# Sparse attention and a Mish MLP on one core: half of batch 0's strided q and k loaded as fp32 by SyncE, local v behind them, batch 1's local v cast in flight, and the loads of every block held behind a mark

## Chip, cores and metric

The kernel runs on one core of one Trainium2 chip. The metric is the device time of one execution in microseconds. TensorE is called PE, VectorE DVE, ScalarE ACT, GpSimd POOL and SyncE SP. ACT and SP issue hardware DMAs, which copy without a change of type. POOL issues software DMAs, which in this kernel also cast fp32 to bf16 in flight.

## The reference, cut to what matters

```python
# q, k, v: (8 batches, 8 heads, 576 positions, 64) in fp32
rel = pos[:, None] - pos[None, :]
mask_local   = (rel >= 0) & (rel < 32)                                  # heads 0 to 3
mask_strided = (rel >= 0) & (pos[None, :] % 32 == pos[:, None] % 32)    # heads 4 to 7
attn_out = softmax(where(mask, q @ k.T / 8, -1e9)) @ v

# x: attn_out as (4608 tokens, 512); w_in: (512, 2048); w_out: (2048, 512)
h = x @ w_in
g = h * tanh(softplus(h))        # Mish
out = g @ w_out                  # (4608, 512) in fp32
```

## The kernel before

Attention goes by batches of 576 positions, the MLP by nine blocks of 512 tokens (`t` = 0 to 8). Attention of batch `t + 1` is woven into the second matmul (`w_out`) of block `t`, one step of a list after each step of the MLP. The order of all instructions is written out by hand (`manual_schedule`), so on each engine, and on each engine's DMA queue, program order is execution order. Semaphores keep the data right.

Strided heads lie as 72 partitions of 8 positions, local heads as 96 positions in each of 6 windows. A local window also needs the 32 positions before it, so `vl` holds 128 partitions a window: 96 of its own and 32 that repeat the end of the window before. q and k are needed with the head dimension on partitions. Batches 0 and 1 transpose them on PE (`t_step`), batches 2 to 7 by DMA transposes that SP issues (`transpose_by_dma`, lines L224 and L230: one each for strided k and q, `kTs` and `qTs`, then two each for local k and q, `kTl` and `qTl`, the last of them writing `qTl`).

**Start.** SP loads strided k of heads 4 and 5 as fp32 into `st0`, which DVE casts, and local v of heads 0 and 1 as fp32 into `vl32` (L868, L871), which POOL casts (L898). POOL's queue loads, with a cast in flight, the other strided k heads, all strided q, strided v, local k and q (L126, L154, L147), then local v of heads 2 and 3 (L893), the first two quarters of `w_in` (L184), and, behind the cast of v and a memset (L899), the last two quarters. PE runs `unread` matmuls, whose results nobody reads, between the first transposes. When the strided scores, the local scores and the local products with v (`pv2`, L369) are through, the dense matmuls of block 0 (L522) begin.

**Block 0.** POOL goes on with `w_out` and batch 1's q, k and strided v. SP loads batch 1's local v as fp32 (L171) once a small `gate` DMA, which reads the third quarter of `w_in`, could be issued (L940); POOL casts it during the second half of the block.

**Blocks 1 to 7.** The first matmul (`mlp1`) is seven products of quarters in place of eight (lines L553, and L522 for the rest), the second as well (L749). In the step `fourth` of block `t`, POOL issues the loads of the next batch's local v (`load_own_v_loc`, four DMAs, L175), then strided v of batch `t + 2`, and at the first step of the second matmul strided k and q of batch `t + 2` (L126). In block 1 alone POOL first copies four elements of `qTl` to `mark` (L628): it waits there for the last DMA transpose of batch 2, and the loads wait behind it. ACT copies the 32 repeated rows of v from the window before (`share_v_loc`, L181) at the eighth step of the second matmul. Late in the block POOL casts local k and q of batch `t + 2` (L199), which SP loaded as fp32 (L140), and SP transposes them. POOL also masks the local scores (L353).

Of the kernel before, what the change touches and what calls it, by code (L numbers as in the profile page):

```python
# [10 lines left out]
F32 = mybir.dt.float32  # L11
# [5 lines left out]
NW = 6  # L17
# [3 lines left out]
CS, PN = 8, 72  # L21
# [22 lines left out]
def kernel(ctx, tc, q, k, v, moe_w_in, moe_w_out, out):  # L44
    nc = tc.nc
    B, H, S, D = q.shape
# [78 lines left out]
    def load_str(b, dst, src, h0=0):  # L125
        nc.gpsimd.dma_start(  # L126
            dst[b % 2][0:PN, h0:4, :], src[b, 4 + h0:8].rearrange("h (p j) d -> p h (j d)", j=CS)
        )
# [47 lines left out]
                vl[b % 2][32:128, :, h, 0:D], v[b, h].rearrange("(w p) d -> p w d", p=WQ)  # L176
            )

    def share_v_loc(b):
        x = vl[b % 2]  # L180
        nc.scalar.copy(x[0:32, 1:NW, :, 0:D], x[96:128, 0:NW - 1, :, 0:D])  # L181

    def load_w_in(f0, f1):
        nc.gpsimd.dma_start(  # L184
            w_in[:, :, f0:f1], moe_w_in.rearrange("(cc p) f -> p cc f", p=128)[:, :, f0:f1]
        )
# [8 lines left out]
    def cast(eng, out_, in_):  # L195
        if eng is nc.scalar:
            nc.scalar.copy(out_, in_)  # L197
        else:
            eng.tensor_copy(out_, in_)  # L199

    def load_tiles_loc(b, dst, src):
        to = by_tile(dst[0])
        for h in range(4):
            nc.gpsimd.dma_start(
                to[:, h // 2, :, h % 2, :], src[b, h].rearrange("(i p) d -> p i d", p=PL)
            )
# [38 lines left out]
    def t_step(b, kind, which, hp, eng=None):  # L245

        eng = eng or nc.vector
        tr = tile_t("tr")[:].bitcast(BF16)
        if kind == "s":
            src = (qs if which == "q" else ks)[b % 2]  # L250
            for u in range(8):
                h, jj = 2 * hp + u // 4, u % 4
                nc.tensor.transpose(
                    tr[:, PN * u:PN * u + PN],
                    src[0:PN, h, 128 * jj:128 * jj + 128],
                    ident[0:PN, 0:PN],
                )
            dst = (qTs if which == "q" else kTs)[:, 8 * SU * hp:8 * SU * hp + 8 * SU]
            cast(
                eng, dst.rearrange("c (u n) -> c u n", u=8)[:, :, 0:PN],  # L260
                tr[:, 0:S].rearrange("c (u n) -> c u n", u=8),
            )
        else:
            src = by_head((ql if which == "q" else kl)[b % 2])
            for j in range(CL):
                for e in range(2):
                    nc.tensor.transpose(  # L267
                        tr[64 * e:64 * e + 64, PL * j:PL * j + PL],
                        src[:, 2 * hp + e, D * j:D * j + D], ident[0:PL, 0:PL],
                    )  # L270
            dst = qTl[:, hp, :] if which == "q" else kTl[:, hp, 32:32 + S]
            cast(
                eng, dst.rearrange("c (p j) -> c p j", j=CL),
                tr[:, 0:S].rearrange("c (j p) -> c p j", j=CL),
            )

    def unread(n, i_acc=None):

        tr = tile_t("un")[:] if i_acc is None else acc(i_acc, "un")[:, 0, :]
        for _ in range(n):  # L280
            nc.tensor.matmul(tr, lhsT=zeros[:, 0:128], rhs=zeros, start=True, stop=True)
# [224 lines left out]
    def mlp1(t, accs):  # L506
# [83 lines left out]
        y = {}  # L590
# [28 lines left out]
        def fourth():  # L619
            product(z[2], 0, a22, t4, last=True)  # L620
            for n in range(2):
                mish(z[2][n], 1, 0, 2 * n)
            if t == 1:
                sums_w()[2](slice(4, 8))
                sums_w()[3](slice(0, 4))
            sums_g(gT, 0, 4, "12")
            if t == 1:
                Po.tensor_copy(mark[:], qTl[0:1, 1, S - 4:S])  # L628
            if t < B - 1:
                load_own_v_loc(t + 1)  # L630
            if t < B - 2:
                load_early_v_str(t + 2)
# [228 lines left out]
    with tc.manual_schedule():  # L861
# [1 line left out]
        Sc.preload_act_table(AF.Exp)  # L863
        Sc.dma_start(consts[:], consts_h.ap())
        st0 = g_pool.tile([128, 16, 512], BF16, tag="gT", name="st0")
        st0 = st0[0:PN].rearrange("p a b -> p (a b)").bitcast(F32)[:, 0:1024].rearrange("p (h x) -> p h x", h=2)
        nc.sync.dma_start(st0, k[0, 4:6].rearrange("h (p j) d -> p h (j d)", j=CS))
        nc.sync.dma_start(vl32[32:128, 0, 0, :], v[0, 0, 0:96, :])  # L868
        first = v[0, 0:1, 0:1, :].offset + 64 * D
        heads = vl32[:].rearrange("p h w d -> p (h w) d")  # L870
        nc.sync.dma_start(heads[:, 1:12, :], bass.AP(v.tensor, first, [[D, 128], [WQ * D, 11], [1, D]]))  # L871
        load_str(0, ks, k, 2)
        load_str(0, qs, q)
        load_early_v_str(0)
        load_early_loc(0)
        Dv.memset(zeros, 0.0)
# [8 lines left out]
        for i in range(2):  # L885
            Dv.memset(vs[i][:, :, :, D:D + 1], 1.0)
            Dv.memset(vl[i][:, :, :, D:D + 1], 1.0)
        for i in range(2):
            Dv.memset(vl[i][0:32, 0, :, D:D + 1], 0.0)

        for h in (2, 3):
            first = v[0, h:h + 1, 0:1, :].offset - 32 * D
            nc.gpsimd.dma_start(  # L893
                vl[0][:, :, h, 0:D], bass.AP(v.tensor, first, [[D, 128], [WQ * D, NW], [1, D]])
            )
        load_w_in(0, 512)
        load_w_in(512, 1024)
        cast(Po, vl[0][:, :, 0:2, 0:D], vl32[:, 0:2].rearrange("p h w d -> p w h d"))  # L898
        Po.memset(vl[0][0:32, 0, :, 0:D], 0.0)  # L899
        load_w_in(1024, 1536)  # L900
        load_w_in(1536, 2048)
        for x in (ks, qs):
            Po.memset(x[1][64:SU].rearrange("p h x -> p (h x)").bitcast(F32), 0.0)

        a = Attn(0)
        unread(16)
        cast(Dv, ks[0][0:PN, 0:2, :], st0)
        t_step(0, "s", "k", 0, Sc)
        unread(3, 2)
        t_step(0, "s", "k", 1, Sc)  # L910
        ps = [a.bias("s", i, i) for i in range(2)]
        unread(5, 2)
        t_step(0, "s", "q", 0, Sc)
        t_step(0, "s", "q", 1, Dv)
        unread(2, 2)
        ps.append(a.bias("s", 2, 2))
# [19 lines left out]
        load_early_v_str(1)  # L936
        load_w_out(1, 2)
        load_early_loc(1)
        load_w_out(2, 4)
        nc.sync.dma_start(gate[:], w_in[0:1, 0, 1024:1280])  # L940
        load_v_loc(1)
        accs = (1, 0, 2)
        gT, g1s, g1 = mlp1(0, accs)
        a.pv2("l", 0, 1)
# [17 lines left out]
        for t in range(NBLK):  # L962
            if t == 0:
                x, y, z = accs
                at, ts = attn_steps(1, y, y)
                at[3] += [
                    lambda: load_early_v_str(2), lambda: load_tiles_loc(2, kl, k),
                    lambda: cast_v_loc(1, Po), lambda: load_tiles_loc(2, ql, q),
                ]
                at[12].append(lambda: transpose_by_dma(2))  # L970
                at[1].append(lambda: sums_w()[0](lo))
                at[7].append(lambda: sums_w()[0](hi))
                at[9].append(lambda: sums_w()[1](lo))
                at[11].append(lambda: sums_w()[1](hi))
                at[14].append(lambda: sums_x(1, "1"))
                at[15] += [
                    lambda: spread_v_str(2, Dv),
                ]
                out_accs = (z, x)
            else:  # L980
                if t == 1:
                    split_third()
                x, y = 0, 1
                gT, z, g1 = mlp1(t, (y, x) if t == 1 else (x, y))
                at = attn_steps(t + 1, x, y) if t + 1 < B else []
                if t == 1:
                    at[0].append(lambda: sums_w()[3](hi))
                if t + 2 < B:
                    at[10].append(lambda: transpose_by_dma(t + 2))
                if t + 1 < B:  # L990
                    at[7].append(lambda: share_v_loc(t + 1))
                if t + 2 < B:
                    at[0].append(lambda: load_qk_str(t + 2))
                if t + 1 < B:
                    at[12].append(lambda: sums_x(t + 1, "1"))
            for i, g in enumerate(g1):
                g()
                if t == 0:
                    for s in ts if i == len(g1) - 1 else ():
                        s()  # L1000
                    continue
            if t == 0:
                steps = mlp2(t, gT, out_accs, fc_major=True)
            elif t == NBLK - 1:
                mlp2_last(t, gT, z[5])
                break
            else:
                za, zc = [bank(i, "pso")[:].rearrange("p (n o) -> p n o", n=2) for i in range(2)]
                steps = mlp2_seven(t, gT, z[5], za, zc)
                if t + 1 == B:  # L1010
                    steps[12] = lambda f=steps[12]: (sums_x(t + 1, "1"), f())
            for i, g in enumerate(steps):
                g()
                if i < len(at):
                    for s in at[i]:
                        s()
                if t > 0 and i == 9 and t + 2 < B:
                    cast_qk_loc(t + 2, Po, Po)
            if t < B - 3:
                load_qk_loc(t + 3)  # L1020
# [30 lines left out]
```

## Time and profile before

| | |
|---|---|
| median of 3 runs | 288.06 us (287.17 to 288.32) |
| the profiled execution | 290.55 us, span 288.8 us |
| PE busy | 279.3 us, 97% of the span |
| PE weight loads, ACT, DVE, POOL busy | 219.3, 196.6, 190.8, 105.3 us |
| granted clock of PE | 0.993 on the mean |
| DMA | 40.73 MB, 141 GB/s; HBM read 37.20 MB, written 9.44 MB |
| packets under 512 bytes | 86396 of 103965 |

Times in the profile are from the start of the span. Block `t` begins with its first dense matmul: block 0 at 21.6, block 1 at 57.4, block 2 at 86.5, block 3 at 119.9 us. A row of the timeline has start, length, engine, line, operation, what it writes and reads, how often, and in brackets how long the engine had been idle and what ended that. A row of DMA issues has the size that one DMA writes and the time from issue to landing. In the DMA view q0 is POOL's software queue and q1 SP's hardware queue, with packets, MB written and the share of the 16 engines' time that their packets took; these overlap, so a share can pass 100%.

### The profile page before, as it was taken

Reading aid. Unit: us, or ns where it says so; the run is one execution under the profiler, and the core shown is the slowest. Engines: PE = TensorE matmul, PEld = TensorE weight load, DVE = VectorE, ACT = ScalarE, POOL = GpSimd, SP = SyncE. Lnnn points to the kernel's source line nnn. Section 1 sums busy time; section 2 is a strip of 40 time slices with the busy share of each in tenths; the row PEclk is TensorE's granted clock in tenths of the full one; section 3 lists DMA queues with packets and bytes.
Section 4 is the critical chain, followed back from the end, with each engine's and each line's share of the span. In section 5 each row is a group of like instructions: output and inputs, shape, how many; then the busy total and the mean of one; then the engine's idle time right before and its main releaser. Section 6 shows DMA issues by size and latency. Waiting matters only on the chain.

```text
span 288.8 us, 7515 instructions
## 1 busy us (share of the span) xinstructions
PE 279.3 (97%) x3106; PEld 219.3 (76%) x3121; DVE 190.8 (66%) x403; ACT 196.6 (68%) x292; POOL 105.3 (36%) x122
## 2 busy tenths in 40 slices
PE   8999999999999969999999999999999999999995
PEld 3564455686898648977898889778977897788684
DVE  2273167889786737768776777687868776735742
ACT  2578643699857947689758985898589858506920
POOL 8375536307396015910691069306710600000000
PEclk9999999999999979999999999999999999999999
DMA  8999999999979999999999999999993032003004
GB/s 158 185 205 190 193 194 199 145 137 241 171 102 116 130 257 160 144 235 152 161 109 123 218 151 139 143 227 151 160 149 113 1 137 47 0 3 145 0 2 145
DMA packets 103965, 40.73 MB, mean 141 GB/s; under 512 B 86396, under 2 KB 99436, under 8 KB 103932
## 3 DMA queue, kind: packets, MB, share of 16 engines
q1 hardware_dynamic: 67900, 25.13, 57.1%
q0 software_dynamic: 35744, 14.87, 46.8%
q8 instruction: 24, 0.39, 0.6%
q10 hardware_dynamic: 288, 0.25, 0.3%
q14 instruction: 9, 0.07, 0.1%
HBM read 37.20 MB, written 9.44 MB: 162 GB/s over the span
## 4 chain that ended last, share of the span: by engine, by line
PE 87%; DMA 7%; DVE 2%; ACT 1%; POOL 1%; issue 1%; SPq 0%; ACTq 0%; POOLq 0%
PE pso L749 30%; PE psu L553 10%; PE psh L522 9%; PE psv L553 8%; PE psb L553 7%; PE po L369 4%; PE pso L809 4%; PE psb L522 4%; PE pso L782 4%; DMA qTl<-ql 4%; DMA ql<-in_q_dram 4%; PE ps L333 3%; PE trx L418 1%; PE tr L267 1%; DVE x_l L381 1%
## 5 line engine op out<-in xcount | busy, mean ns | idle before, releaser
L353 POOL TENSOR_TENSOR Pl<-Pl,consts_sb 128x960 bf16<-128x960 bf16 (+1 forms) x18 | 29.2, 1635 | 87.1 <-issue 68.5
L749 PEld LDWEIGHTS <-gT 128*128 128x128 bf16 x448 | 41.8, 98 | 5.8
L553 PEld LDWEIGHTS <-w_in 128*128 128x128 bf16 x384 | 37.4, 98 | 8.5
L749 PE MATMUL pso<-w_out,gT 128*128 128x256 bf16 x336 | 40.9, 273 | 0.0
L749 PEld LDWEIGHTS <-Sg 128*128 128x128 bf16 x336 | 32.1, 100 | 5.1
L522 PEld LDWEIGHTS <-w_in 128*128 128x128 bf16 x208 | 20.3, 98 | 16.7 <-issue 0.6
L553 PEld LDWEIGHTS <-Sw 128*128 128x128 bf16 x288 | 28.2, 98 | 3.3
L522 PE MATMUL psh<-xT,w_in 128*128 128x512 bf16 (+1 forms) x127 | 29.0, 365 | 0.8 <-ACT xT L197 0.2
L749 PE MATMUL pso<-Tw,Sg 128*128 128x256 bf16 x224 | 28.0, 281 | 0.0
L197 ACT COPY xT<-trx 128x576 bf16<-128x576 bf16 (+3 forms) x24 | 14.2, 629 | 18.4 <-PE trx L418 13.0
L197 ACT COPY osb<-pso 128x512 f32<-128x512 f32 (+1 forms) x17 | 9.4, 554 | 22.3 <-PE pso L749 12.9
L562 ACT ACTIVATE gT<-psu 128x1024 bf16<-128x1024 f32 x16 | 16.4, 1025 | 8.4 <-PE psu L553 8.4
L657 DVE TENSOR_TENSOR psu<-psb,p 128x512 f32<-128x512 f32 x16 | 11.2, 700 | 13.8 <-PE psb L553 13.0
L395 DVE TENSOR_TENSOR x_s<-po,rden 72x512 bf16<-72x512 f32 x28 | 19.2, 687 | 1.0
L175 POOL DMA_DIRECT2D vl<-in_v_dram x24 | 18.8, 791 | 0.5 <-PE psv L553 0.4
L533 ACT ACTIVATE gT<-psh 128x1024 bf16<-128x1024 f32 x16 | 16.2, 1024 | 3.9 <-PE psh L522 3.8
L657 DVE TENSOR_TENSOR Sg<-gT 128x256 bf16<-128x256 bf16 (+2 forms) x32 | 12.8, 421 | 8.0 <-ACT gT L562 6.7
L553 PE MATMUL psu<-xT,w_in 128*128 128x256 bf16 x128 | 17.9, 272 | 0.0
L347 ACT ACTIVATE Ps<-ps 72x864 bf16<-72x864 f32 (+1 forms) x18 | 14.7, 857 | 4.6 <-PE ps L333 4.6
L726 DVE TENSOR_TENSOR p<-pso,p 128x512 f32<-128x512 f32 x14 | 9.6, 685 | 12.1 <-PE pso L749 12.1
L553 PE MATMUL psb<-Sx,w_in 128*128 128x256 bf16 x128 | 17.2, 272 | 0.0
L522 PE MATMUL psb<-xT,w_in 128*128 128x512 bf16 (+1 forms) x72 | 16.4, 355 | 0.0
(139 smaller groups left out, 593.2 us busy)
## 6 DMA issues: line engine op xcount, KB each, us to landing
out_dram<-osb SPq DMA_DIRECT2D x9, 512.0 KB, 8.0
out_dram<-p SPq DMA_DIRECT2D x7, 512.0 KB, 6.7
kl<-in_k_dram SPq DMA_DIRECT2D x5, 576.0 KB, 10.2
ql<-in_q_dram SPq DMA_DIRECT2D x5, 576.0 KB, 14.2
qs<-in_q_dram POOLq DMA_DIRECT2D x8, 288.0 KB, 13.4
vsr<-in_v_dram POOLq DMA_DIRECT2D x8, 288.0 KB, 9.4
w_in<-in_moe_w_in_dram POOLq DMA_DIRECT2D x4, 512.0 KB, 9.6
w_out<-in_moe_w_out_dram POOLq DMA_DIRECT2D x4, 512.0 KB, 17.9
```

Source lines behind the costliest of these rows:

```text
L175: nc.gpsimd.dma_start(vl[b % 2][32:128, :, h, 0:D], v[b, h].rearrange("(w p) d -> p w d", p=WQ))
L197: nc.scalar.copy(out_, in_)
L347: nc.scalar.activation(pt[0:n, :, 0:nw], ps[0:n, :, o0:o0 + nw], AF.Exp, scale=scale)
L353: meng.tensor_tensor(out=pm, in0=pm, in1=mk[0:n, :].unsqueeze(1).unsqueeze(1).to_broadcast([n, 2, nu, w]), op=ALU.mult,)
L369: nc.tensor.matmul(po[:, h, :], lhsT=pt[0:n, c0:c0 + 128], rhs=rhs, start=True, stop=True,)
L395: nc.vector.tensor_tensor(out=dst.rearrange("p e (h d) -> p e h d", h=4), in0=po[0:m, :, :, 0:D], in1=rden[0:m].unsqueeze(3).to_broadcast( ...
L522: nc.tensor.matmul(ps_u[:, o:o + n], lhsT=w_in[:, cc, fc * 128:(fc + 1) * 128], rhs=xT[:, cc, a:a + n], start=(cc == 2 and (o == 0 or len( ...
L533: nc.scalar.activation(to, tiles[g][:], AF.Mish)
L553: nc.tensor.matmul(p[:, 256 * j:256 * j + 256], lhsT=lhs[:, cc, f:f + 128], rhs=rhs[:, cc], start=(first and j == 0 and cc == 0), stop=(la ...
L562: nc.scalar.activation(gT[:, c:c + src.shape[1], 256 * half_t:256 * half_t + 256], src, AF.Mish,)
L657: nc.vector.tensor_tensor(out=out_, in0=in0, in1=in1, op=op)
L749: nc.tensor.matmul(ps[:, pair, :], lhsT=lhs(c, 128 * pair), rhs=rhs(c), start=(first and pair == 0 and c == 0), stop=(last and c == 7), sk ...
```

## The change

- At the start SP loads strided k and then strided q of heads 4 and 5 as fp32 into `st0`; DVE casts both. POOL loads only heads 6 and 7 of both.
- SP then issues a `gate` DMA that reads POOL's half of `qs`, so it waits for that half to land. Local v of heads 0 and 1 is behind it on SP.
- On POOL, the first quarter of `w_in` goes ahead of local v of heads 2 and 3, and the last two quarters become one DMA.
- The order of the first transposes is k, q of heads 4 and 5, then k, q of heads 6 and 7; there are 11, 2, 1, 1 unread matmuls where there were 16, 3, 5 ahead of them.
- Batch 1's local v is loaded by POOL with the cast in flight (four DMAs), between the third and the fourth part of `w_out`. POOL copies the repeated rows (`share_v_loc`) in place of the cast. SP's gate and load are gone. The repeated rows of the first window of `vl[1]` are zeroed once by DVE.
- Two of batch 2's four local k loads stand ahead of that copy, two behind it.
- The mark is in every block from 1 to 7 that loads a next batch (`t < B - 1`, so blocks 1 to 6; block 7 has none).

```diff
-    def share_v_loc(b):
+    def share_v_loc(b, eng=nc.scalar):
         x = vl[b % 2]
-        nc.scalar.copy(x[0:32, 1:NW, :, 0:D], x[96:128, 0:NW - 1, :, 0:D])
+        cast(eng, x[0:32, 1:NW, :, 0:D], x[96:128, 0:NW - 1, :, 0:D])
...
             sums_g(gT, 0, 4, "12")
-            if t == 1:
+            if t < B - 1:
                 Po.tensor_copy(mark[:], qTl[0:1, 1, S - 4:S])
-            if t < B - 1:
                 load_own_v_loc(t + 1)
             if t < B - 2:
                 load_early_v_str(t + 2)
...
-        st0 = ...bitcast(F32)[:, 0:1024].rearrange("p (h x) -> p h x", h=2)
-        nc.sync.dma_start(st0, k[0, 4:6].rearrange("h (p j) d -> p h (j d)", j=CS))
+        st0 = ...bitcast(F32)[:, 0:2048].rearrange("p (y h x) -> p y h x", y=2, h=2)
+        for i, src in enumerate((k, q)):
+            nc.sync.dma_start(st0[:, i], src[0, 4:6].rearrange("h (p j) d -> p h (j d)", j=CS))
+        load_str(0, ks, k, 2)
+        load_str(0, qs, q, 2)
+        nc.sync.dma_start(gate[:], qs[0][0:1, 2, 0:256])
         nc.sync.dma_start(vl32[32:128, 0, 0, :], v[0, 0, 0:96, :])
...
-        load_str(0, ks, k, 2)
-        load_str(0, qs, q)
         load_early_v_str(0)
         load_early_loc(0)
...
+        load_w_in(0, 512)
         for h in (2, 3):
...
-        load_w_in(0, 512)
         load_w_in(512, 1024)
         cast(Po, vl[0][:, :, 0:2, 0:D], vl32[:, 0:2].rearrange("p h w d -> p w h d"))
         Po.memset(vl[0][0:32, 0, :, 0:D], 0.0)
-        load_w_in(1024, 1536)
-        load_w_in(1536, 2048)
+        load_w_in(1024, 2048)
...
-        unread(16)
-        cast(Dv, ks[0][0:PN, 0:2, :], st0)
+        unread(11)
+        for i, x in enumerate((ks, qs)):
+            cast(Dv, x[0][0:PN, 0:2, :], st0[:, i])
         t_step(0, "s", "k", 0, Sc)
-        unread(3, 2)
+        unread(2, 2)
+        t_step(0, "s", "q", 0, Sc)
+        unread(1, 2)
+        ps = [a.bias("s", i, i) for i in range(2)]
         t_step(0, "s", "k", 1, Sc)
-        ps = [a.bias("s", i, i) for i in range(2)]
-        unread(5, 2)
-        t_step(0, "s", "q", 0, Sc)
+        unread(1, 2)
         t_step(0, "s", "q", 1, Dv)
...
-        load_w_out(2, 4)
-        nc.sync.dma_start(gate[:], w_in[0:1, 0, 1024:1280])
-        load_v_loc(1)
+        load_w_out(2, 3)
+        load_own_v_loc(1)
+        load_w_out(3, 4)
...
-                    lambda: load_early_v_str(2), lambda: load_tiles_loc(2, kl, k),
-                    lambda: cast_v_loc(1, Po), lambda: load_tiles_loc(2, ql, q),
+                    lambda: load_early_v_str(2), lambda: load_tiles_loc(2, kl, k, (0, 1)),
+                    lambda: share_v_loc(1, Po), lambda: load_tiles_loc(2, kl, k, (2, 3)),
+                    lambda: load_tiles_loc(2, ql, q),
```

More of the change, by code (lines that the diff above doesn't have):

```diff
@@ L199, in cast, with load_tiles_loc @@
             eng.tensor_copy(out_, in_)
-    def load_tiles_loc(b, dst, src):
+    def load_tiles_loc(b, dst, src, heads=range(4)):
         to = by_tile(dst[0])
-        for h in range(4):
+        for h in heads:
             nc.gpsimd.dma_start(
@@ L865 @@
         st0 = g_pool.tile([128, 16, 512], BF16, tag="gT", name="st0")
-        st0 = st0[0:PN].rearrange("p a b -> p (a b)").bitcast(F32)[:, 0:1024].rearrange("p (h x) -> p h x", h=2)
-        nc.sync.dma_start(st0, k[0, 4:6].rearrange("h (p j) d -> p h (j d)", j=CS))
+        st0 = st0[0:PN].rearrange("p a b -> p (a b)").bitcast(F32)[:, 0:2048].rearrange("p (y h x) -> p y h x", y=2, h=2)
+        for i, src in enumerate((k, q)):
[3 more added lines that the diff above has]
+        nc.sync.dma_start(gate[:], qs[0][0:1, 2, 0:256])
         nc.sync.dma_start(vl32[32:128, 0, 0, :], v[0, 0, 0:96, :])
@@ L887 @@
             Dv.memset(vl[i][:, :, :, D:D + 1], 1.0)
-        for i in range(2):
-            Dv.memset(vl[i][0:32, 0, :, D:D + 1], 0.0)
+        Dv.memset(vl[0][0:32, 0, :, D:D + 1], 0.0)
+        Dv.memset(vl[1][0:32, 0, :, :], 0.0)
+        load_w_in(0, 512)
         for h in (2, 3):
```

## The prediction

> **What bounds the kernel now.** I read first the windows cut at the starts of the token blocks (the first L553 matmul of each, from the chain of waits in order of time), then the timeline where a block was long, then the start, then the DMA view of short stretches. In the windows the columns are length, busy time of PE, PEld, DVE, ACT, POOL, granted clock, DMA share, GB/s; blocks 1, 2 and 3 are
>
> ```profile
> 57.40:86.46 29.06, 29.01 (x350) 24.40 (x349) 24.97 (x50) 24.23 (x36) 14.34 (x16) 1.00 1.24 162
> 86.46:119.90 33.44, 30.72 (x349) 25.26 (x349) 21.49 (x44) 23.40 (x35) 13.92 (x16) 0.95 1.36 164
> 119.90:148.88 28.98, 28.93 (x347) 24.30 (x347) 21.42 (x44) 23.02 (x35) 13.13 (x15) 1.00 1.27 166
> ```
>
> PE is busy all of blocks 1 and 3; blocks 4 to 6 take 28.93, 28.90 and 28.80. Only block 2 is long, 4.5 us over the mean of blocks 3 to 5 (28.94), at a mean clock of 0.95. The timeline shows why:
>
> ```profile
> 65.84 0.71 POOL L628 COPY mark<-qTl 1x4 bf16<-1x4 bf16 x1 [11.46 <-DMA qTl<-ql]
> 85.77 3.25 POOL L175 DMA_DIRECT2D vl<-in_v_dram  x4
> 93.96 2.81 SPq L230 DMA_TRANSPOSE qTl<-ql  x1
> 103.04 0.22 PE L333 MATMUL ps<-qTl,kTl 64*128 64x96 bf16 x2 [1.46 <-DMA qTl<-ql]
> 104.47 0.27 PE L333 MATMUL ps<-qTl,kTl 64*128 64x96 bf16 x2 [1.21 <-DMA qTl<-ql]
> 104.67 3.23 PE L749 MATMUL pso<-Tw,Sg 128*128 128x256 bf16 x16
> ```
>
> In block 1 POOL waited at the mark until batch 2's transposes had landed, and only then loaded. So ks of batch 3, issued at 70.64, landed 13.3 us later and batch 3's transposes began only at 84.00. Block 2 has no mark: its v, ks and qs loads (85.77 to 91) ran beside those transposes, the last of which landed 10.47 us after issue (the median of qTl's landings is 5.3, the shortest 3.0). PE needed it at 101.6, idled, and its next 16 matmuls took 3.23 us where 16 of that kind else take 1.75 to 1.85.
>
> The other stretch that isn't full of useful matmuls is the start, up to 21.62 us. From the chain and the timeline:
>
> ```profile
> 4.34 10.12 DMA ql<-in_q_dram
> ...
> 15.76 0.30 POOL L899 MEMSET vl<- 32x256 bf16 x1 [6.08 <-DMA vl<-in_v_dram]
> 16.21 1.49 POOL L184 DMA_DIRECT2D w_in<-in_moe_w_in_dram  x2 [0.15 <-issue]
> 18.27 0.43 PE L369 MATMUL po<-vl,Pl 128*128 128x65 bf16 x8
> 21.62 2.75 PE L522 MATMUL psh<-xT,w_in 128*128 128x512 bf16 x12
> ```
>
> The last of the POOL loads that attention needs, ql, lands at 14.46 and sets the end; local v was complete at 16.06, 2.2 us before its first reader at 18.27. From there to the dense matmuls is 3.35 us (reciprocals, products, transposes, copies).
>
> **The sum's own time.** The profiled execution took 290.55 us, span 288.8; the median of the runs is 288.06. I take the differences from the trace and put them on the median; on the profiled execution they would start from 290.55.
>
> **The mark in every block.** Removed from block 2 is the traffic beside the transposes. Undisturbed they run: kTs at 84.00, qTs at 85.84 (its data lands then), kTl at some 87.5, three more at 1.3 us spacing (118.07, 119.39, 120.71 in a quieter stretch), so the last issues at 91.4 and lands 3.0 to 5.3 later, at 94.4 to 96.7; PE asks at 101.6. The stall and the slow matmuls go: -4.5 us.
>
> What the mark adds: POOL stands at it until some 95 (8.5 us into block 2; 8.4 in block 1), and queued behind it are the copy and seven DMA issues, 6.2 us as at 65.84 to 72.05. Then POOL is free at 101.5, and its next work, the l2 mask, is due 17.6 us into the block (75.01 in block 1), at 104.1. ACT's share of v stands 22.86 us in (80.26), at 109.3; v's four loads ended 13.1 us after the mark started in block 1, which gives 108.1: covered by 1.2 us. ks landed 18.1 us after the mark, so the next transposes begin at 113, end at 123.5 to 126, and block 3 needs them 15 us after its start at 115.4, at 130.4: covered by 4 to 7 us. One turn of this loop is 18.1 + 10.4 to 12.7 = 28.5 to 30.8 us against a block of 28.94, so it stands or slips by up to 1.9 us a block. I take 0, since block 1's turn had kl and ql of SP ahead of its loads, which in later blocks go out behind the transposes and stores. Upper bound, if it slips in full: from block 4 on ACT's share comes late, some 0.5, 2 and 4 us less 1 us of slack each.
>
> **The start: q, k, local v.** A further 288 KB of fp32 go out on SP ahead of v, 144 KB leave POOL's queue. These are the DMA view's rows of queue, packets and MB, for 12.2 to 14.2 (128-byte packets alone), 16 to 22 (1024-byte alone), 30 to 34 (1024-byte beside SP's 256-byte) and 71 to 76 (128-byte beside 256-byte):
>
> ```profile
> q0 software_dynamic: 1438, 0.36, 184.5%
> ...
> q0 software_dynamic: 1210, 1.20, 123.0%
> ...
> q0 software_dynamic: 705, 0.60, 89.8%
> q1 hardware_dynamic: 704, 0.18, 31.9%
> ...
> q0 software_dynamic: 2309, 0.30, 96.6%
> q1 hardware_dynamic: 1975, 0.50, 79.1%
> ```
>
> So POOL's queue moves 0.2 MB/us alone, 0.15 beside SP's small packets, which take turns with its own. Without 144 KB (0.7 us) and without v's small packets at 5 to 7 (some 0.4 us), ql lands at 13.3, qs's half at 8.5 (10.02 less 0.7 of data and 0.8 of queue). The strided scores come 2 us earlier, but ql's transposes follow its landing, so PE asks for local v at 18.27 - 1.1 = 17.2. The gain comes from the time before POOL's first data packets, which the profile has near 4.7, in which SP has the engines alone. The Trainium skill, "DMA: Bandwidth & Descriptors", Rules for kernel authors, says that spreading transfers over issuing engines doesn't help, since all share the same 16; by that ql would gain only v's 0.4, and the rival in which the start gains (below) would reach 283.2 instead of 282.5. No row here shows a half moved from POOL to SP; that SP's big packets alone read as fast as POOL's casts (0.82 MB in 104 to 106, against 1.20 MB written from twice as much read in 16 to 22) agrees with the shared bound.
>
> Local v is what is late next. Its two SP loads now stand behind the gate, which waits for qs's half. By 8.5 + 0.8 + 0.4 (the issue spacings at 22.91 to 23.71 and 1.25 to 1.64) they are out at 9.7. How soon an SP transfer starts behind a full POOL queue is shown once: in 22.9 to 27 all 758 packets are POOL's, although this stood issued since 22.91:
>
> ```profile
> gate<-w_in SPq DMA_DIRECT2D x1, 0.5 KB, 5.4
> ```
>
> So v's 1504 packets start between 10.9 (1.2 us after issue, as st0's did) and 13.4; I take 12.8, nearer the gate's row, since POOL's queue is as full. Then 1 us beside the end of w_in's first quarter (176 packets/us), which now stands ahead of heads 2 and 3, and 1330 packets beside the 1536 of those heads at 857/us together: 3.1 us. At 16.9 both are about done, landed at 18.0; POOL's wait, cast (0.85) and memset (0.30) end at 19.4. Local attention starts 1.1 us later than before: +1.1 us. Bounds: all covered, -1.1; v's packets get fewer turns and drag on beside w_in's second quarter at 176/us, complete at 21.4, +3.1.
>
> **Clock.** PE would idle from 17.2 to 19.4. In block 2 it had idled from 101.6 to 104.5 but for two short matmuls, and the granted clock, the third number from the end, went to 0.50 for 3.4 us:
>
> ```profile
> 103.00:104.00 1.00, 0.22 (x2) 0.09 (x1) 0.60 (x1) 0.00 (x0) 0.00 (x0) 0.99 1.29 217
> 104.00:105.00 1.00, 0.53 (x4) 0.48 (x5) 0.00 (x0) 0.26 (x1) 0.00 (x0) 0.50 1.02 399
> ```
>
> So 2.9 us was enough. For 2.2 us I take 0; from 2.9 on (v complete at 20.1) some 0.7, since DVE sets the pace of the 3.35 us behind it. The Trainium skill, "TensorE: Matmul & The Clock Gate", Part 1, puts the drop behind an idle window of about 3.4 us; by it the price would fall due only from v complete at 20.6. The trace's 2.9 decides.
>
> **The rest.** w_in's second half is one DMA, issued behind that memset, at 19.4. Its 1024 packets at 0.2 MB/us (5.2 us), some 1.5 to start and 1.9 to land, give 28.0; group 4, which follows ACT's L533 at 27.87, asks at 27.8 + 1.1 = 28.9. Taken as 0; if the cover goes, up to +1. Batch 1's v: 3072 small packets leave SP (19 us in which POOL's queue lost 0.05 MB/us, 4.7 us of it), 2304 of 128 bytes come to POOL (3.2 us at 719/us). That pays back the late start before w_out and ks, qs are due, and no PE wait on w_out is in the list of waits: 0. Four issues (0.74 each) and the share for two casts on POOL lie where POOL waits for landings: 0, at most +0.5 if ql of batch 2 slips. Five unread matmuls fewer lie in front of transposes that now come sooner: 0.
>
> Sum: -4.5 + 1.1 = -3.4; 288.06 - 3.4 = 284.7.
>
> **Rivals.** *Slower: local v decides the start.* For it: the gate's 5.4 us for 0.5 KB. v complete at 21.4 or later costs 3.1, the clock 0.7, w_in's second half 1 more: +4.8 against -4.5, 288.4; each further us adds itself, and the point where it decides is v complete at 21.1. Against: heads 2 and 3 have short packets, beside which SP's move fast. Chance 0.15, times 286.7 to 290. *The hold stalls later blocks:* as above, +1.5 to +6 on the forecast, 286.2 to 290.7. Against: nothing in block 1 waits. Chance 0.12. *The start gains:* v lands before PE asks and ql's 1.1 us count: 288.06 - 4.5 - 1.1 = 282.5 to 283.5. Against: the 4 us in which SP moved nothing. Chance 0.13. *Nothing changes in block 2,* because the stall came from SP's own order and not from POOL's loads: 288.06 + 1.1 = 289.2. Against: landings of 8 to 13 us with 2194 POOL packets between 85.6 and 92, against 3 to 5 at 114 to 121. Chance 0.05.
>
> **How the numbers follow.** The forecast has 0.55, with 283.5 to 286.6 as its own range. What a measurement here can tell from no change is about 0.5%, 1.44 us, so the limits are 286.6 and 289.5. Faster: 0.55 + 0.13, and 0.04 from the near ends of the first two rivals: 0.72. Same: 0.10 from the middle of those two and 0.05: 0.15. Slower: what is left of them, 0.13. The range 282.9 to 288.6 leaves out the far ends of both sides.
>
> **What would show it.** Block 2 at 29 us, with no PE wait on qTl and no 0.50 in the clock after 5 us; marks in six blocks, each 8 to 11 us into its block. At the start: qs tr near 9, ql tr near 13.3, POOL's L899 memset near 19, first po<-vl near 19.4, dense psh near 22.7. A dense start past 25, an ACT share waiting for vl, or a block 2 above 31 would make the prediction wrong.

## The result and the profile after

The changed kernel is slower: 291.43 us median (290.55 to 292.62, 4 runs) against 287.86 us (287.17 to 288.32, 4 runs), a ratio of 1.0116, 95% interval 1.0076 to 1.0156. The forecast was 284.7 us. Here and below medians are of all runs, while ratios leave out executions that were over 1.5% longer than the kernel's quickest, among them one of 480.35 us of `after_warm` and one of 357.22 us of `v_on_pool`. The profiled execution took 291.14 us, span 289.4. It starts block 1 at 61.78, where the profiled execution of before started it at 57.40.

The windows of the changed kernel, cut at the starts of blocks 1, 2 and 3 (same columns as before):

```profile
61.78:90.84 29.06, 29.06 (x351) 24.40 (x349) 25.01 (x50) 24.24 (x36) 13.61 (x15) 1.00 1.41 168
90.84:119.90 29.06, 29.06 (x350) 24.39 (x349) 21.50 (x44) 23.18 (x35) 13.31 (x15) 1.00 1.18 159
119.90:148.90 29.00, 29.00 (x348) 24.32 (x347) 21.43 (x44) 23.02 (x35) 13.31 (x15) 1.00 1.27 173
```

Block 2 is 29.06 us, with PE busy throughout. Its mark, from POOL's timeline, shows what holds the loads:

```profile
97.37 0.18 POOL L628 COPY mark<-qTl 1x4 bf16<-1x4 bf16 x1 [7.14 <-DMA qTl<-ql]
```

POOL waited 7.14 us and went on 6.5 us into the block. So block 2, on which the forecast lived, looks in this profile as forecast, and the time is nevertheless longer: it went at the start. From the timeline of 6 to 26 us (SPq is SP's sequencer, issuing a DMA; rows left out are marked with dots):

```profile
8.15 0.62 SPq L870 DMA_DIRECT2D gate<-qs  x1
...
9.44 0.43 SPq L874 DMA_DIRECT2D vl<-in_v_dram  x1
...
19.24 0.83 POOL L199 CAST vl<-vl 128x768 bf16<-128x768 f32 x1 [10.84 <-DMA vl<-in_v_dram]
20.13 0.30 POOL L900 MEMSET vl<- 32x256 bf16 x1
20.39 0.75 POOL L184 DMA_DIRECT2D w_in<-in_moe_w_in_dram  x1
20.49 0.60 PE L369 MATMUL po<-vl,Pl 128*128 128x65 bf16 x8 [3.54 <-POOL vl L900]
...
22.74 1.90 PE L522 MATMUL psh<-xT,w_in 128*128 128x512 bf16 x4
```

PE idled 3.54 us for local v; POOL had stood for 10.84 us at the cast, because SP's second load of v, issued at 9.44, landed 9.67 us later. Windows of single microseconds around it show a second price, in the granted clock (third number from the end):

```profile
18.00:19.00 1.00, 0.00 (x0) 0.00 (x0) 0.00 (x0) 0.00 (x0) 0.00 (x0) 1.00 1.29 204
...
20.00:21.00 1.00, 0.51 (x10) 0.51 (x10) 0.00 (x0) 0.00 (x0) 0.94 (x3) 0.50 0.26 41
...
25.00:26.00 1.00, 1.00 (x10) 0.69 (x8) 0.00 (x0) 0.85 (x2) 1.00 (x3) 0.50 1.13 209
...
27.00:28.00 1.00, 1.00 (x7) 0.44 (x5) 0.00 (x0) 0.63 (x1) 0.99 (x2) 1.00 1.05 186
```

The clock was 0.50 from 19.8 to 26.6 us. The row of 20 to 21 also shows the DMA engines at a share of 0.26: the second half of `w_in` could only be issued behind the memset, at 20.39.

### The profile page after: what moved, and what is told of

It reads as the page before. It is cut to its first block, busy times and chain, and to the rows that moved or that the text cites. A ratio compares the mean times of both kernels' runs of the same rounds, so it can differ in the third digit from the quotient of the medians.

```text
span 289.4 us, 7521 instructions
## 1 busy us (share of the span) xinstructions
PE 279.9 (97%) x3112; PEld 219.6 (76%) x3112; DVE 192.8 (67%) x404; ACT 196.5 (68%) x292; POOL 106.9 (37%) x128
## 3 DMA queue, kind: packets, MB, share of 16 engines
HBM read 37.01 MB, written 9.44 MB: 161 GB/s over the span
## 4 chain that ended last, share of the span: by engine, by line
PE 90%; DMA 5%; DVE 1%; issue 1%; POOL 1%; ACT 1%; SPq 0%; ACTq 0%; POOLq 0%
PE pso L748 30%; PE psh L522 10%; PE psu L553 10%; PE psv L553 8%; PE psb L553 7%; PE psb L522 5%; PE po L369 5%; PE pso L808 4%; PE pso L781 4%; DMA vl<-in_v_dram 3%; PE ps L333 3%; DMA qs<-in_q_dram 2%; PE trx L418 2%; DVE x_l L381 1%; PE tr L267 1%
## 5 line engine op out<-in xcount | busy, mean ns | idle before, releaser
L748 PEld LDWEIGHTS <-Sg 128*128 128x128 bf16 x336 | 31.5, 98 | 4.4
L522 PEld LDWEIGHTS <-w_in 128*128 128x128 bf16 x208 | 20.6, 99 | 17.0 <-issue 1.4
L522 PE MATMUL psh<-xT,w_in 128*128 128x512 bf16 (+1 forms) x136 | 30.8, 379 | 0.0
L748 PE MATMUL pso<-Tw,Sg 128*128 128x256 bf16 x224 | 26.7, 273 | 0.0
L175 POOL DMA_DIRECT2D vl<-in_v_dram x28 | 20.6, 746 | 7.7 <-DMA w_out<-in_moe_w_out_dram 2.3
L562 ACT ACTIVATE gT<-psu 128x1024 bf16<-128x1024 f32 x16 | 16.4, 1025 | 8.4 <-PE psu L553 8.4
L656 DVE TENSOR_TENSOR psu<-psb,p 128x512 f32<-128x512 f32 x16 | 11.2, 700 | 13.4 <-PE psb L553 12.6
L533 ACT ACTIVATE gT<-psh 128x1024 bf16<-128x1024 f32 x16 | 16.2, 1024 | 4.6 <-PE psh L522 4.6
L628 POOL COPY mark<-qTl 1x4 bf16<-1x4 bf16 x6 | 1.8, 301 | 46.6 <-DMA qTl<-ql 46.6
L656 DVE TENSOR_TENSOR Sg<-gT 128x256 bf16<-128x256 bf16 (+2 forms) x32 | 12.8, 422 | 8.0 <-ACT gT L562 6.7
L553 PE MATMUL psb<-Sx,w_in 128*128 128x256 bf16 x128 | 17.2, 272 | 0.0
## 6 DMA issues: line engine op xcount, KB each, us to landing
kl<-in_k_dram SPq DMA_DIRECT2D x5, 576.0 KB, 13.3
vsr<-in_v_dram POOLq DMA_DIRECT2D x8, 288.0 KB, 8.4
ks<-in_k_dram POOLq DMA_DIRECT2D x7, 288.0 KB, 10.1
qs<-in_q_dram POOLq DMA_DIRECT2D x7, 288.0 KB, 11.5
```

Of the source, the lines that this page charges most:

```text
L175: nc.gpsimd.dma_start(vl[b % 2][32:128, :, h, 0:D], v[b, h].rearrange("(w p) d -> p w d", p=WQ))
L522: nc.tensor.matmul(ps_u[:, o:o + n], lhsT=w_in[:, cc, fc * 128:(fc + 1) * 128], rhs=xT[:, cc, a:a + n], start=(cc == 2 and (o == 0 or len( ...
L533: nc.scalar.activation(to, tiles[g][:], AF.Mish)
L553: nc.tensor.matmul(p[:, 256 * j:256 * j + 256], lhsT=lhs[:, cc, f:f + 128], rhs=rhs[:, cc], start=(first and j == 0 and cc == 0), stop=(la ...
L562: nc.scalar.activation(gT[:, c:c + src.shape[1], 256 * half_t:256 * half_t + 256], src, AF.Mish,)
L656: nc.vector.tensor_tensor(out=out_, in0=in0, in1=in1, op=op)
```

## Experiments

Two theories were tried. By the first, the late local v costs more than forecast. By the second, the 4.5 us that the holds were to bring were not in the median of before, only in its profiled execution, which took 290.55 us where the three timed runs took 287.17 to 288.32. Both hold, and each is about half of the error.

### Before again, and the marks alone

Two further profiled executions of the unchanged kernel, `before_again` and `before_third`, and a kernel that has nothing of the change but the marks, `marks_only`:

```diff
-            if t == 1:
-                Po.tensor_copy(mark[:], qTl[0:1, 1, S - 4:S])
             if t < B - 1:
+                Po.tensor_copy(mark[:], qTl[0:1, 1, S - 4:S])
                 load_own_v_loc(t + 1)
```

> The kernel before, unchanged, profiled once more. Theory 1 (block 2's 4.5 us stall belongs to some executions only, the first profiled one among them; at 290.55 us that one stood 2.2 to 3.4 us over every timed run): block 2 takes 29 to 31.5 us here, the span is 285 to 287.5. Theory 2 (the stall is in every execution, and the profiled one was long for another reason): block 2 again 33 to 34 us, span 288 to 289.

> The kernel before with nothing but the mark in blocks 1 to 6. Start and block 0 stay as before, dense matmuls at 21.6 us. Theory 1: block 2 is 29 us in the profile, but the timed runs gain little, 0 to 1.5 us, since the median run of before had little of the stall. Theory 2: the timed runs gain 4 to 4.5 us, 283.5. If the hold itself costs something in the blocks, one of blocks 2 to 6 is over 29.3 us.

> The kernel before, profiled a third time. If block 2's stall belongs to some executions: block 2 at 29 to 30 us or, less likely, 31 to 34, and the profiled time moves with it; the other blocks as always.

Block 2 in the windows of `before_again`, which took 287.31 us:

```profile
86.85:116.36 29.51, 29.18 (x349) 24.49 (x349) 21.48 (x44) 23.29 (x35) 13.22 (x15) 1.00 1.37 165
```

of `before_third`, 286.35 us:

```profile
86.48:115.54 29.06, 29.06 (x351) 24.38 (x349) 21.50 (x44) 23.18 (x35) 12.82 (x15) 1.00 1.38 161
```

and of `marks_only`, 287.15 us in that execution:

```profile
86.86:115.92 29.06, 29.01 (x349) 24.38 (x349) 22.36 (x44) 23.18 (x35) 13.30 (x15) 1.00 1.21 166
```

The same program has a block 2 of 33.44, 29.51 or 29.06 us. In `before_again` the last transpose was late as well, but PE lost only 0.45 us:

```profile
92.23 10.02 DMA qTl<-ql
```

That line is from its chain of waits: issued 1.7 us earlier than in the first profile (93.96), with nearly the same landing (10.02 against 10.47). PE's need is fixed, so the stall is the small difference of two large numbers, and varies from execution to execution. Timed, `marks_only` is 286.78 us (286.48 to 287.44, 12 runs) against 288.01 us (286.62 to 292.23, 23 runs), ratio 0.9957 (0.9932 to 0.9982). The marks are worth 1.2 us in the median. The quickest runs hardly differ (286.62 and 286.48), so what goes is the spread above them: over the three series of runs of before on three chips, 11 of 75 took 290 us or more, and none of the 12 of `marks_only` took over 287.44. The granted clocks of these runs agree: 9 of the 75 have 0.993 or 0.994 on the mean, as the first profiled execution (0.993), and all nine took 290.1 us or more, while 64 of the 65 with 0.998 to 1.000 took less than 290.

### The change without its start, and batch 1's v alone

`start_undone` is the whole change except the start (the loads, casts and transposes of batch 0 as they were); `batch1_v_only` has in addition the mark in block 1 alone, so only batch 1's local v is changed:

```diff
-        load_w_out(2, 4)
-        nc.sync.dma_start(gate[:], w_in[0:1, 0, 1024:1280])
-        load_v_loc(1)
+        load_w_out(2, 3)
+        load_own_v_loc(1)
+        load_w_out(3, 4)
...
-                    lambda: cast_v_loc(1, Po), lambda: load_tiles_loc(2, ql, q),
+                    lambda: share_v_loc(1, Po), lambda: load_tiles_loc(2, kl, k, (2, 3)),
+                    lambda: load_tiles_loc(2, ql, q),
```

> The kernel before with only the part on batch 1's local v (cast in flight on POOL, share on POOL, the order of w_out and of batch 2's local k). Predicted at 0: start as before, block 1 at 57.4 to 57.9, time within 0.7 us of before. If four DMAs more on POOL delay w_out or batch 2's loads: PE waits in block 0 or block 1's transposes end later, 0.5 to 2 us slower.

> The change without its start: batch 0's loads, POOL's order and the unread matmuls as before; batch 1's v cast in flight and the mark in blocks 1 to 6 as in the change. If the start is all that costs: block 1 at 57.4 to 57.9, all later blocks at 29.1 or less, time 1 to 2 us under before, 5 us under the changed kernel. If the hold costs something beside batch 1's v: not faster than before.

> The changed kernel once more, on the chip of the next two, as their measure: 3 to 4 us over before; in the profile first po<-vl at 20 to 21.6 us, a clock of 0.50 behind it, block 1 at 61.5 to 62.5.

`batch1_v_only`: 286.93 us against 287.51, ratio 0.9981 (0.9963 to 0.9999), so a gain of at most some 1 us and perhaps none. It has no mark in block 2, and yet it too had no run above 287.25 in 12; with 15 such runs in a hundred, 12 without one come up one time in seven, so what the tail owes to the mark and what to batch 1's v isn't settled. `start_undone`: 286.97 us (286.67 to 287.54) against 288.0, ratio 0.9962 (0.9941 to 0.9982). The unchanged changed kernel on the same chip, `after_again`: 290.70 us, ratio 1.0078 (1.0053 to 1.0103). The start therefore costs 290.70 - 286.97 = 3.7 us, and everything else gains 1.0; 5 us had been expected for the start.

The two profiles agree. PE's timeline of `start_undone`:

```profile
18.60 0.43 PE L369 MATMUL po<-vl,Pl 128*128 128x65 bf16 x8
...
20.14 1.29 PE L522 MATMUL psh<-xT,w_in 128*128 128x512 bf16 x4
...
21.95 3.40 PE L522 MATMUL psh<-xT,w_in 128*128 128x512 bf16 x15
```

and of the changed kernel (22 to 27 us):

```profile
22.74 1.90 PE L522 MATMUL psh<-xT,w_in 128*128 128x512 bf16 x4
...
25.39 1.86 PE L522 MATMUL psh<-xT,w_in 128*128 128x512 bf16 x5
```

Local attention starts 20.49 - 18.60 = 1.9 us later. From there to the dense matmuls proper it takes 4.90 us in place of 3.35, and the rest of the half-clock time costs another 0.6: block 1 starts at 61.78 in place of 57.73, 4.05 us later, of which 1.9 is the wait for v and 2.2 what follows at half clock.

### PE kept busy in the wait

`after_warm` and `after_warm2` are the same program, the changed kernel with 16 matmuls that nobody reads where PE waits for local v:

```diff
         a.qk([("l", 2)], None, a.bias("l", 2, 2))
+        unread(16)
         load_w_out(0, 1)
```

> The changed kernel with 16 more unread matmuls between the last local scores and the first local products, where PE idles from 17 to 20.5 us. They keep PE busy and move no data. If the start's 4.4 us are 2.2 of waiting for v (first po<-vl at 20.49 against 18.27) and 2.2 of PE at half clock behind the wait: no 0.50 clock, po<-vl still at 20.4 to 20.8, block 1 at 59.4 to 59.8, time 1.8 to 2.4 us under the changed kernel. If the slow clock lies under DVE's work, as the prediction priced it: at most 0.7 us gained.

> The changed kernel with 16 more unread matmuls where PE waits for local v, once more and beside the changed kernel itself. If the slow clock behind the wait costs 2.2 of the start's 4.4 us: no 0.50 clock, block 1 at 59.4 to 59.9, 1.8 to 2.4 us under the changed kernel. If it lies under DVE's work: at most 0.7 us under it.

`after_warm` took 290.13 us on the median of the five runs that its ratio, 1.0114 (1.0076 to 1.0152), is taken from. PE's timeline of `after_warm2`:

```profile
17.00 3.63 PE L281 MATMUL un<-Tw 128*128 128x512 bf16 x16
20.47 0.42 PE L369 MATMUL po<-vl,Pl 128*128 128x65 bf16 x8
...
23.80 6.42 PE L522 MATMUL psh<-xT,w_in 128*128 128x512 bf16 x29
```

Local v is as late as before (20.47), the clock stays at 1.00, and from v to the dense matmuls it is 3.33 us again; block 1 starts at 59.86, 1.9 us sooner than in `after_again` (61.72). Timed it took 289.93 us, ratio 1.0055 (1.0029 to 1.0081), only 0.8 us less than `after_again`, where 1.8 to 2.4 had been expected. The profiled execution, 289.21, was the quickest of its 12 runs, 0.7 under their median, and that of `after_again`, 291.07, was 0.4 over its own, so the profiles' 1.9 overstates what the median gains. By the runs the 3.7 us divide into 0.8 for the clock and 3.0 for the rest (286.97 to 289.93), by the profiles the 4.0 between the starts of block 1 (57.73 and 61.72) divide into 1.9 and 2.1. Which division is nearer stays open: the 16 matmuls end at 20.6 us, so in an execution whose v came earlier they would themselves hold PE back, which no trace here shows. That the clock is in the timed runs too can be seen in `after_again`: two of its 12 runs had a granted clock of 0.992 in place of 0.986 to 0.988 and were with 289.84 and 290.12 us its two quickest.

### What makes v late

Three ways to bring local v in sooner. `after_no_gate` takes the gate away, so that SP issues v right behind strided k and q:

```diff
-        nc.sync.dma_start(gate[:], qs[0][0:1, 2, 0:256])
         nc.sync.dma_start(vl32[32:128, 0, 0, :], v[0, 0, 0:96, :])
```

> The changed kernel without SP's gate DMA, so local v of heads 0 and 1 follows st0 on SP at once; POOL's order is the changed one. If the gate is what makes local v late: v's short packets are through by 7 us, heads 2 and 3 land near 16.6, the first po<-vl is at 17.0 to 17.6, no 0.50 clock, dense matmuls at 20.4 to 21, block 1 at 56.2 to 56.9; time 4.5 to 5.5 us under the changed kernel, about 1 us under before. If w_in's first quarter ahead of heads 2 and 3 is what makes it late: po<-vl still after 18.7, and at most 2 us gained on the changed kernel.

Its timeline at 4 to 26 us:

```profile
10.57 0.31 PEld L253 LDWEIGHTS <-qs 72*128 72x128 bf16 x8 [1.68 <-DMA qs<-in_q_dram]
...
19.97 0.43 PE L369 MATMUL po<-vl,Pl 128*128 128x65 bf16 x8
```

and the DMA view of 5 to 8 us:

```profile
q1 hardware_dynamic: 1317, 0.38, 72.2%
q0 software_dynamic: 296, 0.26, 55.9%
```

PE doesn't wait for v any more, but SP now moves 1317 packets in the 3 us in which POOL's first loads should come in; POOL gets 296, where the changed kernel's POOL moved 713 in the same 3 us. POOL's half of `qs` lands at 10.53 (8.13 with the gate), `ql` at 14.83 (12.71), and local attention still starts at 19.97, where 17.0 to 17.6 had been expected. A part of this is the clock once more. PE, with fewer unread matmuls than before and `qs` late, was busy 1.77 of the 3.41 us up to 11.90, and from there to 15.3 the granted clock was 0.50:

```profile
12.00:13.00 1.00, 1.00 (x25) 0.68 (x22) 0.69 (x1) 0.60 (x1) 0.00 (x0) 0.50 1.29 205
```

The timed runs divide in the same way: five with a mean clock of 0.999 or 1.000 took 287.94 to 288.55 us, five with 0.993 or 0.994 took 288.95 to 289.84. Over all it is 289.05 us (287.94 to 293.55), ratio 1.0025 (0.9985 to 1.0064). That is 3 us better than `after_mark1` of the same series, but no gain over before. In 5 to 8 us POOL moves 588 packets beside SP's k and v (before), 713 behind SP's k and q (changed) and 296 beside all three, less than half. How much of the lateness is the packets and how much the clock wasn't separated.

`after_heads_first` keeps the gate and puts the first quarter of `w_in` back behind local v of heads 2 and 3:

```diff
-        load_w_in(0, 512)
         for h in (2, 3):
...
+        load_w_in(0, 512)
         load_w_in(512, 1024)
```

> The changed kernel with the gate, but heads 2 and 3 of local v ahead of w_in's first quarter on POOL again. If SP's part of v behind the gate is what is late, this makes it worse or leaves it: heads 2 and 3 pass before SP's packets start near 12.3 us, and these then take turns with w_in's 1024-byte packets at 176/us: v complete at 21 to 23, time 0 to 3 us over the changed kernel. If w_in's first quarter ahead of the heads is what delays v: complete near 18.3, 3 to 4.5 us gained.

It is the slowest of all, 292.84 us, ratio 1.0198 (1.0163 to 1.0232). Its PE timeline, and the DMA view of 13 to 18 us:

```profile
22.55 0.60 PE L369 MATMUL po<-vl,Pl 128*128 128x65 bf16 x8 [5.37 <-POOL vl L900]
```

```profile
q0 software_dynamic: 849, 0.79, 94.6%
q1 hardware_dynamic: 716, 0.18, 27.5%
```

The heads on POOL landed at 14.4, four us sooner, but SP's v only at 21.17. Beside `w_in` its 256-byte packets move at 716 in 5 us; from 14 us on, when only `w_in` is beside them, at 616 in 4 us against POOL's 614, 154 per us. In the changed kernel they run beside the heads' 128-byte packets (15 to 17 us):

```profile
q0 software_dynamic: 790, 0.12, 79.7%
q1 hardware_dynamic: 779, 0.20, 74.7%
```

390 per us. In both stretches the two queues have moved as many packets as each other within 2%: read so, they take turns packet by packet, and SP goes at the pace of POOL's packets. So the change's order of POOL's queue was not the cause; it had made v quicker than the old order would.

`after_mark1` is the changed kernel with the mark in block 1 alone (`if t == 1`):

> The changed kernel with the mark in block 1 alone, as before: only the start and batch 1's v are changed. Theory 1: as slow as the changed kernel, 3 to 5 us over before, the start alone accounting for it. Theory 2: 7.5 to 9 us over before (the start's 4.4 and the stall back). In the profile block 1 begins 4.4 us later than before's 57.4 in both.

292.10 us (291.18 to 294.05, 6 runs), ratio 1.0128 (1.0082 to 1.0174). The loss at the start doesn't come from the holds: here local attention starts at 21.61, later than with them. Block 2 stayed at 29.06 even without its mark, block 4 took 30.30 (29.21 in the changed kernel); why block 4 is long was not followed up.

### A version that beats both

`v_on_pool` keeps the change's q, k on SP, its marks and batch 1's v. All four heads of batch 0's local v go on POOL with the cast in flight, behind `ql` and ahead of `w_in`. The gate, SP's loads of v and POOL's cast are gone:

```diff
-        nc.sync.dma_start(gate[:], qs[0][0:1, 2, 0:256])
-        nc.sync.dma_start(vl32[32:128, 0, 0, :], v[0, 0, 0:96, :])
...
-        load_w_in(0, 512)
-        for h in (2, 3):
-            first = v[0, h:h + 1, 0:1, :].offset - 32 * D
+        nc.gpsimd.dma_start(vl[0][32:128, 0, 0, 0:D], v[0, 0, 0:96, :])
+        for h in range(4):
+            w0 = 1 if h == 0 else 0
+            first = v[0, h:h + 1, 0:1, :].offset + (w0 * WQ - 32) * D
...
+        load_w_in(0, 512)
         load_w_in(512, 1024)
-        cast(Po, vl[0][:, :, 0:2, 0:D], vl32[:, 0:2].rearrange("p h w d -> p w h d"))
```

> The changed kernel with SP's local v and the gate taken out: all four heads of batch 0's local v are cast in flight on POOL, behind local q and ahead of w_in's first quarter, so no POOL cast is needed either. SP loads only st0's two halves. ql lands near 12.7 as in the changed kernel; 3072 packets of 128 bytes at 719/us and more follow it, v complete at 15.5 to 16.5; PE asks at 16.9. If local v on SP is the only cost of the change: po<-vl at 17.0, dense matmuls at 20.3 to 20.8, block 1 at 55.9 to 56.6, time 1 to 2 us under before. If w_in's first quarter is then what is late (landing near 18.2 against a need at 18.4): up to 1 us less gained.

Time 286.01 us against 287.51, ratio 0.9954 (0.9930 to 0.9978). PE's timeline:

```profile
17.52 0.43 PE L369 MATMUL po<-vl,Pl 128*128 128x65 bf16 x8
...
19.25 1.18 PE L522 MATMUL psh<-xT,w_in 128*128 128x512 bf16 x4
...
21.23 9.01 PE L522 MATMUL psh<-xT,w_in 128*128 128x512 bf16 x41
```

Local v was complete at 16.37, before PE asked; `ql` landed at 13.63, 1.1 us sooner than in `start_undone` (14.69), and local attention starts 1.1 us sooner. What set that start is told by the chain of waits, which goes back to POOL's `qs` in `start_undone` and to SP's q in `v_on_pool` (start, length, transfer). Of `start_undone`:

```profile
2.21 8.11 DMA qs<-in_q_dram
```

and of `v_on_pool`:

```profile
1.24 5.80 DMA st<-in_q_dram
```

Strided q was there at 10.31 and at 7.04 us, and from there both chains run over the strided scores and DVE's normalizing, not over `ql`. PE began `ql`'s transposes 0.05 us after its landing in both, though, so `ql` had next to nothing to spare, and the two causes aren't separated. Only 0.5 us of the 1.1 reach block 1 (57.21 against 57.73; 55.9 to 56.6 had been expected): local attention to the dense matmuls takes 3.71 us against 3.35, and these up to block 1 35.98 against 35.78. Against before the interval is a clear gain; that it is better than `marks_only` (0.9957) or `start_undone` (0.9962) can't be told from the ratios.

## Why the prediction was wrong

**The sum's base (the step that failed first).** The prediction subtracted 4.5 us, a stall of one profiled execution, from the median of other runs. It named both times, 290.55 and 288.06, and did not ask whether the median held the stall: an execution 2.5 us above the median, and above all three runs shown, has something that they have not. The other two profiles hold 0.45 and 0 us of it, and the marks alone are worth 1.2 us in the median. With the rest of what the change does outside the start, -1.0 was measured for this term in place of -4.5: 3.5 us of the error. (In the timeline that has the 3.23 us of 16 matmuls, others of their kind take 1.91, not 1.75 to 1.85; the 4.5 don't hang on that.)

**The holds cost nothing: right.** The first five marks release POOL 5.6 to 7.5 us into their blocks (8.5 was forecast), the sixth 9.2, and blocks 1 to 3 are 29.06, 29.06 and 29.00 us. Block 4 at 29.21 has 0.3 us at most of a slip. The mechanism of the mark was right; its size belonged to one execution.

**The start, first half: right in its times.** `qs`'s half landed at 8.13 (8.5 forecast), `ql` at 12.71 (13.3), and PE asked for local v at 16.95 (17.2). The path to it was another than forecast: PE began `ql`'s transposes at 12.95 without having waited for them, and the one wait of PE that the timeline shows from there to 16.95 is 0.22 us for DVE's normalizing of the strided heads. POOL's queue did get faster when it had less to move and SP's v no longer ran beside it. The Trainium skill, "DMA: Bandwidth & Descriptors", Rules for kernel authors, says that spreading DMAs over issuing engines gives no bandwidth. `v_on_pool`, with k and q on SP, got `ql` 1.1 us sooner than `start_undone` although v as well was on POOL; by that rule the prediction had left 0.4. Rule and runs need not conflict: in 2 to 5 us, when POOL moves next to nothing, SP moved as much in before (0.54 MB, k and v) as in `v_on_pool` (0.51 MB, k and q), and v then came behind `ql`. So the gain can be one of order, of what goes first, and not of bandwidth. No run moves q alone, so this stays argued.

**Local v, +1.1: too small.** SP's first packets were forecast at 12.8 and came at 12.1, 27 of them by 12.6. The rate of 857 packets per us for both queues was too high: 1307 and 1393 packets in 13 to 17 us are 675 per us together. In 15 to 17 us it was 785; ahead of that the larger packets of `w_in`'s first quarter were beside it longer than forecast, till some 14.5 us and not 13.8. First use came at 20.49, not 19.4, which makes +1.9 over `start_undone`.

**Clock, 0: the wrong side of its own threshold.** The prediction had the price fall due from 2.9 us of idle PE on, forecast 2.2, and 3.54 came. The 2.9 was misread as well: in its row of 103 to 104 us the clock is 0.99, so it fell at the end of that row, 2.4 us after 101.6 and with two matmuls in between. That left 0.2 us to the forecast, not 0.7. The late case was then priced at 0.7, since DVE was to set the pace of the 3.35 us behind it. They became 4.90: at half clock PE's part was the longer. With what came after, 1.9 to 2.2 us in the profiles, 0.8 in the timed runs. The Trainium skill, "TensorE: Matmul & The Clock Gate", Part 1, describes free-running windows of 3.41 us and a drop after an idle one. The length agrees: the half clock lasted from 19.80 to 26.62, two such windows. That the window before the drop must have been wholly idle does not: 3.41 us back from 19.80 is 16.4, and PE worked until 16.95; in `after_no_gate` it worked 1.77 of the 3.41 us before the drop.

**`w_in`'s second half: right.** Issued at 20.39, landed at 28.41 (28.0 forecast); DVE waited 4.1 us for it (the list of waits), PE did not.

**Batch 1's v, 0: right within what can be measured** (0.9981, up to 1.0).

**The rivals.** "Local v decides the start" had the mechanism. It was to decide from v complete at 21.1, and v was complete at 20.43; the point was wrong because it was set against 4.5 us of gain and a clock at 0.7, and its range up to 290 ended below the 291.43 that came. By an estimate from the measured terms, v complete later than some 19.6 (18.60 and the 1.0 us gained elsewhere) loses. The sum of what was measured, -1.0 + 3.7 = +2.7 us, is what the last series gives (290.70 against 288.00); the first comparison gave +3.6. Against the forecast's -3.4 the +2.7 are 6.1 us of error: 3.5 from the base and 2.6 from the start, where 3.7 came in place of 1.1.

## What to carry to other kernels

When the profiled execution is slower than the timed median, look for the stall that makes it so, and take nothing from a sum for removing that stall until a second profile shows it again. When one of two queues is relieved, follow the load that was moved behind: here it had one packet for each of the other queue's beside it, and behind a busy POOL queue its first packet came some 3 us after issue. A wait of PE on the path is priced with the clock: here, by the profiles, 1.9 us of late v drew 1.9 to 2.2 us of half-clock work behind it, by the timed runs 0.8. And when loads come at other times, look whether PE still has enough work ahead of them: in `after_no_gate` the clock fell at the start without any wait for v.

## What the runs showed of the hardware

SP DMAs issued while POOL's queue was moving data moved nothing for some 3 us: in the DMA view of 9 to 12 us of the changed kernel only POOL's queue has packets, though the gate was issued at 8.15 and the loads of v at 8.82 and 9.44; SP's first packets came at 12.1 (right columns: count, size, us to landing).

```profile
q0 software_dynamic: 769, 0.61, 129.4%
...
vl<-in_v_dram SPq DMA_DIRECT2D x1, 352.0 KB, 9.7
vl<-in_v_dram SPq DMA_DIRECT2D x1, 24.0 KB, 5.7
```

Once it moved, it had one packet for each of POOL's in two stretches with packets of different sizes: 390 per us beside 128-byte packets (779 against 790), 154 beside 1024-byte ones (616 against 614). That isn't always so: in 5 to 8 us of `after_no_gate` SP moved 1317 to POOL's 296. What keeps SP's packets back before they start, POOL's queue or the gate ahead of them, was not tried.

The granted clock fell to 0.50 behind stretches in which PE was partly busy: of the 3.41 us before the drop PE was busy 0.52 us in the changed kernel (drop at 19.80), 1.24 in the first profile of before (103.97) and 1.77 in `after_no_gate` (11.90). It stayed at 0.50 for 3.4 us in the last two and 6.8 in the first.
